# Softmax reciprocals of an attention stage: from TensorE transposes to a VectorE block transpose and a trip through HBM

## The chip, the core and the metric

The kernel runs on one core of a Trainium2 chip. The metric is the device time of one execution in microseconds (us); the number given for a kernel is the median of its runs. The engines are named as the profile names them: PE (TensorE, matrix products and transposes), PEld (its weight loads), DVE (VectorE), ACT (ScalarE), POOL (GpSimd) and SP (SyncE, which here only issues DMAs). PSUM is the memory that TensorE writes to, SBUF the memory of all engines, HBM the memory off the core.

## The reference, cut to what matters

Causal attention over 2 batches of 12 heads (448 tokens, 64 features a head), its output taken as an 896 x 768 matrix into two feed-forward blocks. Of the attention:

```
scores = where(mask, -1e9, scale * q @ k.T)
attn   = exp(scores - max(scores))
attn   = attn / (sum(attn) + 1e-9)
out    = attn @ v
x      = out with the heads side by side      # 896 x 768
```

Then `(sigmoid(x w_gate) * (x w_val)) w_out` (d_ff 1536), and a second block with softmax, a layer norm and two more products. The change touches only the division by `sum(attn) + 1e-9`.

## The kernel before, in words

**Stages.** Attention comes first, then the first feed-forward block (loops over 12 blocks of `d_ff` at L625 and 6 blocks of features at L659), then the second (7 blocks of 128 tokens). All products are of float32 split into a high and a low part, three products for one.

**Attention.** Heads are taken two at a time, 12 pairs. For a pair `p`, PE forms the scores of four query tiles (`sc_mm`, L364: tiles 3 and 0 first, then 2 and 1) in PSUM; DVE takes the row maxima (`sc_max`, L374); ACT takes the exponentials with the row sums in the same instruction (`sc_exp`, L383, line L388 in the profile), each followed by a short instruction that reads the accumulator out. The probabilities `p_t` hold queries on the partitions; PE transposes them in four groups `u` (`tr_mm`, L435, line L439), ACT copies each group to `pt` as the high part (`tr_hi`, L442, line L446) and DVE subtracts to form the low part (`tr_lo`, L448, line L231). PE multiplies with `v` (`pv_mm`, L457, line L470). The result `x` has features on the partitions and queries along the free axis.

**The division.** It is made on that result, so each query's reciprocal has to stand in a row, repeated over the 64 features of its head. POOL adds 1e-9 to the sums (`sums`, L391, line L393), DVE takes the reciprocals of a 128 x 8 block (`recips`, L396), POOL spreads each over 64 columns (`rs_wide`, L401; line L225, tile `rx`), PE transposes the four blocks of 128 x 128 into PSUM (`rs_mm`, L406; line L411, tile `r`), ACT copies them to SBUF (`rs_out`, L413; line L223, tile `rb`), and DVE multiplies (`x_mul`, L474). ACT and POOL then split the product into high and low parts (`x_hi`, `x_lo`).

**What sets the order.** It is written out by hand. `STEPS` (L515) is a table of entries (step, engine, function, and optionally the first pair and the end of the range). One pair begins every 8 steps, and the loop at L578 runs at each step `s` the entries of PE ('E'), then a piece of the first feed-forward block where it can be had (`early_tiles`), then ACT ('A'), DVE ('D') and POOL ('P'), within an engine in the order of the table. An engine executes in this order and waits on semaphores. At one step `s = 8k` DVE meets entries of three pairs: step 16 of pair k-2 (`tr_lo` of group 3), step 0 of pair k (`sc_max` of tiles 3 and 0), and one step later the reciprocals of pair k-1. ACT at that step has `tr_hi` of group 3, `rs_out`, `x_hi`, and at step `8k+1` the exponential of tile 3 of the new pair.

**DMA.** All DMAs are issued by SP, in program order: `load_qk` (two pairs ahead, after POOL's `prep_k_lo`), `load_v` (after `prep_v_lo`), and the weights (`dma_next`) at steps 8 and 12 and again from step 95 on.

Of the kernel before, what the change touches and what calls it, by code (L numbers as in the profile page):

```python
# [10 lines left out]
F32 = mybir.dt.float32  # L11
# [8 lines left out]
B, H, S, D = 2, 12, 448, 64  # L20
# [3 lines left out]
NQ = 4  # L24
QE = [64, 192, 320, 448]
# [7 lines left out]
EPS_SUM = 1e-9  # L33
# [10 lines left out]
def attn_moe_moe2(ctx: ExitStack, tc: tile.TileContext, qk, v, w_gv, w_out, w_in2, w_out2, g_ln, out):  # L44
# [3 lines left out]
    nc = tc.nc  # L48
# [145 lines left out]
    with ExitStack() as actx:  # L194
# [1 line left out]
        qks = actx.enter_context(tc.tile_pool(name="qks", bufs=2, side="right"))  # L196
        one = actx.enter_context(tc.tile_pool(name="one", bufs=1, side="right"))
        ptp = actx.enter_context(tc.tile_pool(name="ptp", bufs=2, side="right"))
        st = actx.enter_context(tc.tile_pool(name="st", bufs=2, side="right"))
        xfp = actx.enter_context(tc.tile_pool(name="xfp", bufs=2, side="right"))  # L200
        ps_t = actx.enter_context(tc.tile_pool(name="ps_t", bufs=2, space=PSUM, reuse_waits="tile"))
        ps_x = actx.enter_context(tc.tile_pool(name="ps_x", bufs=2, space=PSUM, reuse_waits="tile"))
        ps_s = actx.enter_context(tc.tile_pool(name="ps_s", bufs=2, space=PSUM, reuse_waits="tile"))
# [17 lines left out]
        def on(eng, out, in_):  # L221
            if eng == 'A':
                nc.scalar.copy(out=out, in_=in_)  # L223
            elif eng == 'P':
                nc.gpsimd.tensor_scalar(out=out, in0=in_, scalar1=1.0, scalar2=1.0, op0=ALU.mult, op1=ALU.mult)  # L225
            else:
                nc.vector.tensor_copy(out=out, in_=in_)
# [72 lines left out]

        v3 = [one.tile([128, 2, 2 * D], FR, name=f"v3_{i}") for i in range(2)]
        sum_t = [one.tile([128, 16], F32, name=f"sum{i}") for i in range(3)]
        p_t = [one.tile([128, POFF[NQ]], F32, name=f"p{i}") for i in range(2)]

        mx0 = [one.tile([128, 2], F32, name=f"mx{e}") for e in range(2)]
# [19 lines left out]
        load_v(1)  # L325
        zeros(1)

        rs_t, rx_t, rb_t, pt_t, ps_sc, ps_both, ps_tr, ps_pv, ps_rr, xf_t = {}, {}, {}, {}, {}, {}, {}, {}, {}, {}


        def sc_mask(p, g):
# [57 lines left out]
                                         func=AF.Exp, bias=mx, scale=1.0, accum_out=sm)  # L389

        def sums(p):  # L391
            rs = rs_t[p] = st.tile([128, 16], F32, tag="rs", name="rs")
            nc.gpsimd.tensor_scalar(out=rs[:, 8:16], in0=sum_t[p % 3][:, 0:8], scalar1=EPS_SUM, scalar2=0.0,  # L393
                                    op0=ALU.add, op1=ALU.add)

        def recips(p):  # L396
            nc.vector.reciprocal(out=rs_t[p][:, 0:8], in_=rs_t[p][:, 8:16])

        def rs_wide(p):  # L401
            rx = rx_t[p] = st.tile([128, NQ, 2, D], F32, tag="rx", name="rx")
            r = rs_t.pop(p)[:, 0:8].rearrange("p (a i) -> p i a", a=2)
            on('P', rx, r.unsqueeze(3).to_broadcast([128, NQ, 2, D]))

        def rs_mm(p):  # L406
            ps = ps_rr[p] = ps_x.tile([128, 512], F32, tag="x", name="r")[:, :S]
            rx = rx_t.pop(p).rearrange("p i a d -> p i (a d)")
            for i in range(NQ):

                nc.tensor.transpose(ps[:, max(QE[i] - 128, 0):max(QE[i], 128)], rx[:, i], ident if i else identx)  # L411

        def rs_out(p):  # L413
            rb_t[p] = xfp.tile([128, S], F32, tag="rb", name="rb")
            on('A', rb_t[p], ps_rr.pop(p))


        def tr_blocks(u):

# [70 lines left out]
        def early_tiles():  # L490
# [25 lines left out]
            (0, 'E', lambda p: sc_mm(p, (0, 1)), 3), (2, 'E', lambda p: sc_mm(p, (1,)), 2, 3),  # L516
            *((9 + 2 * u, 'E', lambda p, u=u: tr_mm(p, u), int(u < 2)) for u in range(4)),
            *((13 + n, 'E', lambda p, n=n: pv_mm(p, n)) for n in range(len(CHUNKS))),
            (15, 'E', rs_mm),
            (16, 'A', lambda p: tr_hi(p, 3)), (16, 'A', rs_out), (24, 'A', x_hi, 0, NPR - 1), (22, 'A', x_hi, NPR - 1),  # L520
            (1, 'A', lambda p: sc_exp(p, (3,), (0,)), 2),
            (9, 'A', lambda p: tr_hi(p, 0), 1),
            (1, 'A', lambda p: sc_exp(p, (3,), (1,)), 2), (2, 'A', lambda p: sc_exp(p, (0,)), 2),
            (12, 'A', lambda p: tr_hi(p, 1), 1), (5, 'A', lambda p: sc_exp(p, (2,)), 1),
            (14, 'A', lambda p: tr_hi(p, 2)), (6, 'A', lambda p: sc_exp(p, (1,)), 1),
            (-1, 'D', lambda p: sc_max(p, 3, 0), 2, 3),
            (16, 'D', lambda p: tr_lo(p, 3)), (0, 'D', lambda p: sc_max(p, 3, 0), 3),
            (-7, 'D', prep_q_lo, 3), (9, 'D', recips),
            (2, 'D', lambda p: sc_max(p, 2), 2), (11, 'D', lambda p: tr_lo(p, 0), 1), (3, 'D', lambda p: sc_max(p, 1), 2),
            (13, 'D', lambda p: tr_lo(p, 1)), (21, 'D', x_mul), (15, 'D', lambda p: tr_lo(p, 2)),  # L530
            (8, 'P', sums, 1), (9, 'P', prep_v_lo, 1), (25, 'P', x_lo, 0, NPR - 1), (23, 'P', x_lo, NPR - 1),
            (10, 'P', rs_wide),
            (-10, 'P', prep_k_hi, 3), (-9, 'P', prep_q_hi, 3), (-4, 'P', prep_k_lo, 3), (7, 'P', prep_v_hi, 1),
        )

        sc_mm(0, (0, 1))
# [41 lines left out]
        for s in range(PER * NPR + 26):  # L578
            steps(s, 'E')
            for _ in range(2):  # L580
                if s >= PER * NPR and left and next(early):
                    left -= 1
            steps(s, 'A')
            steps(s, 'D')
            steps(s, 'P')
            if s in (8, 12):
                dma_next()

            for c in range(2 * NE + 2):
                e = s - 88 - 8 * c  # L590
                if e in (3, 5, 7):
                    next(bits_now)
                if e == 8 and c < 2 * NE:
                    chunk_hi(c)
                if e == 9 and c < 2 * NE:
                    chunk_lo(c)
                if e == 0:
                    bits_now = bits_steps(c)
                    next(bits_now)
# [237 lines left out]
```

## Time and profile before

| | |
|---|---|
| median of 3 runs (lowest, highest) | 493.98 us (493.77, 493.98) |
| the profiled execution, its own time | 493.84 us |
| its span, first to last instruction | 492.1 us |
| PE busy, share of the span | 486.2 us, 99% |
| DVE, ACT, POOL busy | 329.0, 225.7, 125.4 us |
| granted TensorE clock, mean | 1.000 |
| DMA packets, data | 12996, 52.79 MB |

The span leaves out some 1.7 us of the execution's own time. A busy PE is a PE with at least one matmul in flight by the profile's model of their ends, so 99% does not say that PE is what the rest waits for; that has to be read from the waits. The attention stage takes the first 105 us or so.

### The profile page before, as it was taken

The page shows a single profiled execution, that of the slowest core. Times are in us where ns is not written, and L with a number is a line of the kernel's source. Part 1 is how long each engine was busy: PE and PEld are TensorE (multiplying, and loading weights), DVE is VectorE, ACT ScalarE, POOL GpSimd, SP SyncE. Part 2 cuts the span into 40 slices and gives each one's busy share as a digit, 9 for nine tenths or more (in the row PEclk, how much of TensorE's full clock was granted, in tenths as well). Part 3 has the DMA queues.
Part 4 walks back from the last instruction along what each step waited for, and adds up shares of the span by engine and source line. Part 5 has one row for each costly group of instructions (what it writes and reads, how often), then busy time and mean ns, then how long its engine had stood idle before and what let it go on. Part 6 is the DMA issues. An engine that isn't in the chain of part 4 may idle for free.

```text
span 492.1 us, 7603 instructions
## 1 busy us (share of the span) xinstructions
PE 486.2 (99%) x2955; PEld 445.6 (91%) x2955; DVE 329.0 (67%) x496; ACT 225.7 (46%) x483; POOL 125.4 (25%) x200
## 2 busy tenths in 40 slices
PE   8999999999999999999999999999999999999997
PEld 7998999899999999999999999999988888899996
DVE  7898888986656778877777746767735987821110
ACT  6988989853433543453453332343321434323111
POOL 5888877610000000000000000000060778510000
PEclk9999999999999999999999999999999999999999
DMA  6722330223332454443344334443331121001001
GB/s 191 249 83 97 93 107 23 65 78 121 124 129 59 156 170 132 168 155 111 121 170 143 114 107 138 162 157 120 132 127 56 74 78 52 1 33 64 33 33 64
DMA packets 12996, 52.79 MB, mean 107 GB/s; under 512 B 1568, under 2 KB 2080, under 8 KB 12960
## 3 DMA queue, kind: packets, MB, share of 16 engines
q1 hardware_dynamic: 12960, 52.31, 32.2%
q8 instruction: 23, 0.38, 0.3%
q14 instruction: 13, 0.11, 0.1%
HBM read 49.55 MB, written 2.75 MB: 106 GB/s over the span
## 4 chain that ended last, share of the span: by engine, by line
PE 82%; ACT 12%; DVE 3%; issue 2%; DMA 1%; POOL 0%; SPq 0%; ACTq 0%; DVEq 0%
PE gv L643 34%; PE pm L673 18%; PE po L766 12%; PE h L705 12%; ACT p L388 7%; ACT pt L446 4%; DVE sum L376 1%; PE gv L502 1%; PE tp L748 1%; DVE pt L231 1%; PE x L470 1%; DMA qkr<-in_qk_dram 1%; PE t L439 1%; PE s L361 1%; PE warm L315 0%
## 5 line engine op out<-in xcount | busy, mean ns | idle before, releaser
L643 PE MATMUL gv<-xy,hl 128*128 128x448 f32 x828 | 168.1, 365 | 0.0
L643 PEld LDWEIGHTS gv<-xy,hl 128*128 128x128 f32 x828 | 155.4, 188 | 12.3
L673 PE MATMUL pm<-g,hl 128*128 128x448 f32 x432 | 87.7, 365 | 0.0
L673 PEld LDWEIGHTS pm<-g,hl 128*128 128x128 f32 x432 | 81.1, 188 | 6.4
L690 POOL TENSOR_SCALAR t<-t,g_sb 128x768 f32<-128x768 f32 x8 | 9.0, 1130 | 247.7 <-PE pm L673 247.7
L134 DVE TENSOR_TENSOR hl<-t,hl 128x768 fp32r<-128x768 f32 x36 | 35.1, 975 | 41.7 <-ACT hl L131 40.0
L766 PE MATMUL po<-wo,lt 128*128 128x384 f32 x336 | 60.6, 339 | 0.0
L705 PE MATMUL h<-wi,xy 128*128 128x512 f32 x252 | 59.3, 396 | 0.0
L766 PEld LDWEIGHTS po<-wo,lt 128*128 128x128 f32 x336 | 58.7, 188 | 0.2 <-POOL wo L695 0.2
L705 PEld LDWEIGHTS h<-wi,xy 128*128 128x128 f32 x252 | 47.1, 187 | 11.4
L117 DVE SCALAR_TENSOR_TENSOR t<-raw,t 128x768 int32<-128x768 int32 (+1 forms) x56 | 52.6, 939 | 1.8
L120 DVE SCALAR_TENSOR_TENSOR t<-raw,t 128x768 int32<-128x768 int32 (+1 forms) x56 | 52.0, 929 | 1.7
L112 ACT ACTIVATE raw<-raw 128x768 f32<-128x768 f32 (+1 forms) x56 | 48.1, 867 | 9.5 <-DMA raw<-in_wo_dram 6.4
L470 PE MATMUL x<-pt,v 128*128 128x384 f32 (+3 forms) x252 | 51.3, 325 | 0.0
L388 ACT ACTIVATE p<-s,sum 128x320 f32<-128x320 f32 (+3 forms) x92 | 43.7, 495 | 10.0 <-DVE sum L376 9.7
L231 DVE TENSOR_TENSOR pt<-t,pt 128x512 fp32r<-128x512 f32 (+1 forms) x48 | 32.2, 671 | 11.2 <-ACT pt L446 11.0
L470 PEld LDWEIGHTS x<-pt,v 128*128 128x128 f32 x252 | 36.9, 190 | 1.6
L171 DVE TENSOR_TENSOR lt<-tp,lt 128x512 fp32r<-128x512 f32 x14 | 9.7, 690 | 36.4 <-ACT lt L170 36.4
L115 DVE TENSOR_SCALAR t<-raw 128x768 int32<-128x768 int32 (+1 forms) x56 | 30.6, 547 | 3.0 <-ACT raw L112 3.0
L131 ACT CAST hl<-t 128x768 fp32r<-128x768 f32 x36 | 30.0, 833 | 4.2 <-PE pm L673 4.2
L183 ACT ACTIVATE wk<-gv 128x448 f32<-128x448 f32 x23 | 11.3, 542 | 44.5 <-PE gv L643 44.5
L446 ACT CAST pt<-t 128x512 fp32r<-128x512 f32 (+1 forms) x48 | 28.3, 590 | 3.1 <-PE t L439 3.1
(101 smaller groups left out, 523.7 us busy)
## 6 DMA issues: line engine op xcount, KB each, us to landing
raw<-in_gv_dram SPq DMA_DIRECT2D x24, 768.0 KB, 4.4
raw<-in_wo_dram SPq DMA_DIRECT2D x20, 768.0 KB, 4.4
raw<-in_wi_dram SPq DMA_DIRECT2D x12, 512.0 KB, 3.5
qkr<-in_qk_dram SPq DMA_DIRECT2D x11, 448.0 KB, 3.3
vr<-in_v_dram SPq DMA_DIRECT2D x12, 256.0 KB, 2.7
out_dram<-o SPq DMA_DIRECT2D x6, 384.0 KB, 2.3
qkr<-in_qk_dram SPq DMA_DIRECT2D x2, 224.0 KB, 2.8
out_dram<-o SPq DMA_DIRECT2D x2, 192.0 KB, 1.9
```

The lines of the kernel that those rows point to most:

```text
L112: nc.scalar.activation(out=w1.bitcast(F32), in_=w1.bitcast(F32), func=AF.Copy, scale=2.0 ** -112)
L117: nc.vector.scalar_tensor_tensor(out=tt, in0=w1, scalar=-2 ** 31, in1=tt, op0=ALU.bitwise_and, op1=ALU.bitwise_or)
L120: nc.vector.scalar_tensor_tensor(out=tt, in0=w0, scalar=29, in1=tt, op0=ALU.logical_shift_right, op1=ALU.bitwise_or)
L134: nc.vector.tensor_tensor(out=lo, in0=t_t.pop(it), in1=f32(hi), op=ALU.subtract)
L231: (nc.gpsimd if eng == 'P' else nc.vector).tensor_tensor(out=out, in0=a, in1=b, op=ALU.subtract)
L388: nc.scalar.activation(out=p_t[p % 2][:, POFF[i] + (1 - e) * n:POFF[i] + (2 - e) * n], in_=ps_sc[p, i][1 - e], func=AF.Exp, bias=mx, scale ...
L446: nc.scalar.copy(out=pt_t[p][:, 0, u, :w], in_=ps_tr[p, u][:, :w])
L470: nc.tensor.matmul(out=ps[:, q0:], lhsT=l, rhs=pt_t[pr][:, c, u, c0:c0 + S - q0], start=(chunk == 0 and n == 0), stop=(chunk == 7 and n == ...
L643: nc.tensor.matmul(out=ps[i, b], lhsT=w[:, a, cs], rhs=xy[kk][:, x, b * S:(b + 1) * S], start=(kk == 0 and a == 0 and x == 0), stop=(kk == ...
L673: nc.tensor.matmul(out=ps[b], lhsT=w[:, a, cs], rhs=g_t[kk][:, x, b * S:(b + 1) * S], start=(kk == 0 and a == 0 and x == 0), stop=(kk == N ...
L705: nc.tensor.matmul(out=h[:, n * 512:(n + 1) * 512], lhsT=xy[kk][:, a, tk], rhs=wi[n * NK + kk][:, c], start=(kk == 0 and i == 0), stop=(kk ...
L766: nc.tensor.matmul(out=ps[n], lhsT=lts[k // 4][:, a, k % 4], rhs=wo[k][:, c, cs], start=(k == 0 and i == 0), stop=(k == NF2 - 1 and i == 2))
```

## The change

It leaves out `rs_wide`, `rs_mm` and `rs_out`, and with them the tiles `rx` and `r` and ACT's copy from `r` to `rb`. In their place DVE, right behind the reciprocal, transposes a 128 x 32 block (8 columns of reciprocals, 24 of zeros) in four blocks of 32 x 32. Row c of each 32-row block then holds the reciprocals of column c for 32 queries. SP writes them to an HBM tile of 8 rows of 128 floats, one DMA for each block (8 rows of 128 bytes), and reads the tile back with two DMAs, one for each head of the pair, each the same 448 floats to 64 partitions. `rb` is written by these DMAs. In `STEPS`, `recips` moves from step 9 to step 8 and to the front of DVE's entries there, so that it stands ahead of `tr_lo` of group 3; `sums` moves from step 8 to the end of step 7 on POOL, which leaves POOL's order as it was; and a new engine key 'S' for SP runs behind DVE and ahead of POOL at each step.

```diff
-        st = actx.enter_context(tc.tile_pool(name="st", bufs=2, side="right"))
+        drm = actx.enter_context(tc.tile_pool(name="drm", bufs=2, space=bass.MemoryType.DRAM))
...
+        rs_in, rs_t, rs_q = ([one.tile([128, n], F32, name=f"rs{n}{o}{i}") for i in range(2)]
+                             for n, o in ((8, "i"), (32, "t"), (32, "q")))
+        for i in range(2):
+            nc.gpsimd.memset(rs_t[i], 0.0)
...
         def sums(p):
-            rs = rs_t[p] = st.tile([128, 16], F32, tag="rs", name="rs")
-            nc.gpsimd.tensor_scalar(out=rs[:, 8:16], in0=sum_t[p % 3][:, 0:8], scalar1=EPS_SUM, scalar2=0.0,
+            nc.gpsimd.tensor_scalar(out=rs_in[p % 2], in0=sum_t[p % 3][:, 0:8], scalar1=EPS_SUM, scalar2=0.0,
                                     op0=ALU.add, op1=ALU.add)
 
         def recips(p):
-            nc.vector.reciprocal(out=rs_t[p][:, 0:8], in_=rs_t[p][:, 8:16])
-
-
-
-        def rs_wide(p):
-            rx = rx_t[p] = st.tile([128, NQ, 2, D], F32, tag="rx", name="rx")
-            r = rs_t.pop(p)[:, 0:8].rearrange("p (a i) -> p i a", a=2)
-            on('P', rx, r.unsqueeze(3).to_broadcast([128, NQ, 2, D]))
-
-        def rs_mm(p):
-            ps = ps_rr[p] = ps_x.tile([128, 512], F32, tag="x", name="r")[:, :S]
-            rx = rx_t.pop(p).rearrange("p i a d -> p i (a d)")
-            for i in range(NQ):
-
-                nc.tensor.transpose(ps[:, max(QE[i] - 128, 0):max(QE[i], 128)], rx[:, i], ident if i else identx)
-
-        def rs_out(p):
+            nc.vector.reciprocal(out=rs_t[p % 2][:, 0:8], in_=rs_in[p % 2])
+            nc.vector.transpose(out=rs_q[p % 2], in_=rs_t[p % 2])
+
+        def rs_rows(p):
+            rows = rd_t[p] = drm.tile([2 * NQ, 128], F32, tag="rd", name="rd")
+            for b in range(0, 128, 32):
+                nc.sync.dma_start(out=rows[:, b:b + 32], in_=rs_q[p % 2][b:b + 8])
+
+        def rs_bcast(p):
             rb_t[p] = xfp.tile([128, S], F32, tag="rb", name="rb")
-            on('A', rb_t[p], ps_rr.pop(p))
-
+            rows = rd_t.pop(p).rearrange("(a i) r -> a (i r)", a=2)[:, D:]
+            for a in range(2):
+                nc.sync.dma_start(out=rb_t[p][a * D:(a + 1) * D], in_=rows[a:a + 1].to_broadcast([D, S]))
...
-            (15, 'E', rs_mm),
-            (16, 'A', lambda p: tr_hi(p, 3)), (16, 'A', rs_out), (24, 'A', x_hi, 0, NPR - 1), (22, 'A', x_hi, NPR - 1),
+            (16, 'A', lambda p: tr_hi(p, 3)), (24, 'A', x_hi, 0, NPR - 1), (22, 'A', x_hi, NPR - 1),
...
-            (16, 'D', lambda p: tr_lo(p, 3)), (0, 'D', lambda p: sc_max(p, 3, 0), 3),
-            (-7, 'D', prep_q_lo, 3), (9, 'D', recips),
+            (8, 'D', recips), (16, 'D', lambda p: tr_lo(p, 3)), (0, 'D', lambda p: sc_max(p, 3, 0), 3),
+            (-7, 'D', prep_q_lo, 3),
...
-            (8, 'P', sums, 1), (9, 'P', prep_v_lo, 1), (25, 'P', x_lo, 0, NPR - 1), (23, 'P', x_lo, NPR - 1),
-            (10, 'P', rs_wide),
-            (-10, 'P', prep_k_hi, 3), (-9, 'P', prep_q_hi, 3), (-4, 'P', prep_k_lo, 3), (7, 'P', prep_v_hi, 1),
+            (9, 'P', prep_v_lo, 1), (25, 'P', x_lo, 0, NPR - 1), (23, 'P', x_lo, NPR - 1),
+            (8, 'S', rs_rows), (9, 'S', rs_bcast),
+            (-10, 'P', prep_k_hi, 3), (-9, 'P', prep_q_hi, 3), (-4, 'P', prep_k_lo, 3), (7, 'P', prep_v_hi, 1), (7, 'P', sums, 1),
...
             steps(s, 'D')
+            steps(s, 'S')
             steps(s, 'P')
```

## Rows read from the trace of the kernel before

**Rows 1.** The page: busy time of each engine, share of the span.

```profile
PE 486.2 (99%) x2955; PEld 445.6 (91%) x2955; DVE 329.0 (67%) x496; ACT 225.7 (46%) x483; POOL 125.4 (25%) x200
```

**Rows 2.** The waits: us in total, times, longest us.

```profile
ACT p L388 <- DVE sum L376: 9.7, 9, 1.1
...
ACT p L388 <- DVE rs L397: 0.3, 1, 0.3
```

**Rows 3.** The chain of waits, 46.5 to 50 us: start us, us, what.

```profile
47.10 0.64 DVE pt L231
```

**Rows 4.** The timeline of ACT, one turn: start us, us, ... [idle before <-releaser].

```profile
46.37 0.22 ACT L388 ACTIVATION_READ_ACCUMULATOR p<-s,sum 128x1 f32 x1
46.46 0.60 ACT L446 CAST pt<-t 128x512 fp32r<-128x512 f32 x1
46.93 0.57 ACT L223 COPY rb<-r 128x448 f32<-128x448 f32 x1
...
49.10 0.64 ACT L388 ACTIVATE p<-s,sum 128x448 f32<-128x448 f32 x1 [1.14 <-DVE sum L376]
```

**Rows 5.** The timeline of DVE, the same turn.

```profile
47.10 0.69 DVE L231 TENSOR_TENSOR pt<-t,pt 128x512 fp32r<-128x512 f32 x1 [0.60 <-ACT pt L446]
47.71 1.28 DVE L376 TENSOR_REDUCE sum<-s 128x2 f32<-128x896 f32 x2
48.91 1.11 DVE L252 SCALAR_TENSOR_TENSOR qks<-qkr,qks 128x448 fp32r<-128x448 f32 x1
49.95 0.19 DVE L397 RECIPROCAL rs<-rs 128x8 f32<-128x8 f32 x1
50.06 0.77 DVE L376 TENSOR_REDUCE sum<-s 128x2 f32<-128x640 f32 x1
```

**Rows 6.** The timeline of POOL, the same turn.

```profile
46.67 0.26 POOL L393 TENSOR_SCALAR rs<-sum 128x8 f32<-128x8 f32 x1 [0.60 <-ACT p L388]
47.01 1.44 POOL L231 TENSOR_TENSOR v<-vr,v 128x384 fp32r<-128x384 f32 x2
48.40 1.14 POOL L231 TENSOR_TENSOR xy<-xf,xy 128x448 fp32r<-128x448 f32 x1
```

**Rows 7.** The timeline of PE, the same turn.

```profile
45.90 0.27 PE L411 MATMUL r<-identx,rx 128*128 128x128 f32 x1
...
46.43 0.26 PE L348 MATMUL s<-mk_r,mk_l 64*128 64x64 bf16 x6
```

**Rows 8.** The timeline of PE, the last pair's transposes.

```profile
100.42 0.27 PE L411 MATMUL r<-identx,rx 128*128 128x128 f32 x1
...
100.77 0.65 PE L502 MATMUL gv<-xy,hl 128*128 128x448 f32 x2
```

**Rows 9.** The timeline of DVE in the second block: two short dependent instructions.

```profile
392.42 0.14 DVE L719 TENSOR_SCALAR st<-st 128x1 f32<-128x1 f32 x1
392.59 0.16 DVE L720 RECIPROCAL st<-st 128x1 f32<-128x1 f32 x1
```

**Rows 10.** Groups of DVE's instructions by line, 0 to 140 us: count | busy us, mean ns.

```profile
L288 DVE CAST mk_l<-two 128x64 bf16<-128x64 f32 x1 | 0.2, 195 | 0.0
```

**Rows 11.** The timeline of DVE, pair 0: its reciprocal and its multiplication.

```profile
14.15 0.19 DVE L397 RECIPROCAL rs<-rs 128x8 f32<-128x8 f32 x1
...
21.25 0.61 DVE L476 TENSOR_TENSOR xf<-x,rb 128x448 f32<-128x448 f32 x1
22.76 0.69 DVE L231 TENSOR_TENSOR pt<-t,pt 128x512 fp32r<-128x512 f32 x1 [0.90 <-ACT pt L446]
```

**Rows 12.** The timeline of SP's queue: the first two weight loads.

```profile
14.15 0.90 SPq L100 DMA_DIRECT2D raw<-in_gv_dram  x2
```

**Rows 13.** The page's DMA issues: count, KB each, us to landing.

```profile
raw<-in_gv_dram SPq DMA_DIRECT2D x24, 768.0 KB, 4.4
...
vr<-in_v_dram SPq DMA_DIRECT2D x12, 256.0 KB, 2.7
...
out_dram<-o SPq DMA_DIRECT2D x2, 192.0 KB, 1.9
```

More of the change, by code (lines that the diff above doesn't have):

```diff
@@ L326, in attn_moe_moe2 @@
         zeros(1)
-        rs_t, rx_t, rb_t, pt_t, ps_sc, ps_both, ps_tr, ps_pv, ps_rr, xf_t = {}, {}, {}, {}, {}, {}, {}, {}, {}, {}
+        rd_t, rb_t, pt_t, ps_sc, ps_both, ps_tr, ps_pv, xf_t = {}, {}, {}, {}, {}, {}, {}, {}
         def sc_mask(p, g):
```

## The prediction

> **What bounds the kernel now.** The page comes first: PE is busy for 99% of the span [rows 1], so taking four transposes a pair off it looks like a gain. But that counts a matmul as busy until its modelled end, so I went to the waits. In the attention stage it is not PE that others wait for: the wait that returns is ACT's exponential, 9.7 us in 9 waits for DVE's maxima and a tenth for DVE's reciprocal [rows 2]. The chain of waits then runs over DVE and ACT alone between 46.5 and 50 us; DVE's subtraction for `pt` (L231, `tr_lo` of group 3) stands on it [rows 3].
>
> One turn, read off the timelines. ACT's cast of group 3 runs from 46.46 to 47.06; DVE has been idle for 0.60 us for it and starts `tr_lo` at 47.10, then the maxima of the next pair's tiles 3 and 0 (47.71 to 48.99), and ACT, idle for 1.14 us, starts that pair's exponentials at 49.10 [rows 4, 5]. From there to the next cast of group 3 ACT is in one piece. So a turn is ACT's run plus the 2.0 us of DVE between cast and exponential; there are ten, one for each of pairs 2 to 11, one for each of the ten waits [rows 2]. `rb`'s copy stands between the cast and ACT's 1.14 us of idle time [rows 4] and only shortens the latter, and the chain never meets the transposes. Whatever goes onto DVE between 47.06 and 49.10 lengthens the turn; what leaves PE, ACT or POOL doesn't shorten it.
>
> Now what the moved reciprocal waits for. ACT has read out the last sum at 46.59; POOL waited 0.60 us for that and adds the epsilon from 46.67 to 46.93 [rows 4, 6]. So the sums reach DVE inside its idle 0.60 us, but near its end.
>
> **The change part by part.**
>
> *Removed.* Four transposes a pair on PE, 0.53 us from the first to the next matmul (45.90 to 46.43) [rows 7]; the copy on ACT, 46.93 to the next start at some 47.4 [rows 4]; the spreading on POOL. In the turns all of these cost or give nothing: ACT waits for DVE behind them anyway, DVE's maxima start as `tr_lo` lets them, and POOL idles ahead of its sums. If PE's cover went, the maxima at 47.71 would wait for the scores; with less work on PE they come earlier. In the last pair PE runs without a pause and its four transposes hold it from 100.42 to 100.77 [rows 8]: -0.35 us.
>
> *Moved: the reciprocal, to the front of DVE's entries at step 8k, and added: the block transpose.* The hand-over between engines takes 0.04 (ACT to DVE, 47.06 to 47.10) to 0.08 us (ACT to POOL, 46.59 to 46.67) [rows 4, 5, 6]; with 0.06 the reciprocal starts at 46.99 and ends 0.19 later, at 47.18 [rows 5]. The transpose reads what it wrote; of two such dependent instructions the second starts 0.03 us after the first's end (392.56 to 392.59) [rows 9], so 47.21. How long a block transpose holds DVE no row shows. A reciprocal of 8 columns lets the next instruction go 0.11 us after its start (49.95 to 50.06) [rows 5], a cast of 64 columns takes 0.195 in all [rows 10]. The transpose has 32 columns. I take 0.11, because between 8 and 64 columns the whole duration hardly changes, and keep as ends 0.11 with no wait for the reciprocal at all and 0.30 (the cast and half as much again for filling a block before it drains). `tr_lo` then starts at 47.21 + 0.11 = 47.32 instead of 47.10: **+0.22 us a turn** (ends +0.11: 46.99 + 0.22 = 47.21; and +0.41). Ten turns: +2.2 us (+1.1 to +4.1). By the Trainium skill (VectorE: DVE Perf Modes, The three transpose paths) VectorE takes 311 ns for 128 x 128 of bf16 in such blocks; less 96 columns that is an estimate of 0.21 us in all, 0.13 to the next start, and the sum would be 0.2 us higher; no row here shows one.
>
> Behind the moved instructions on DVE wait `tr_lo`, both maxima and through them ACT's exponential, which is what I have counted. Where the reciprocal stood before, DVE gains 0.11 us [rows 5]. That is beside ACT's run, except in the last turn, where the exponential was released by the reciprocal [rows 2]: -0.1 us.
>
> In the first turn DVE is late by pair 0's transpose (its reciprocal ends at 14.34 with DVE's next work close behind [rows 11]) rather than by pair 1's; I count it once.
>
> *Added: six DMAs a pair on SP.* SP issues a DMA every 0.45 us when nothing holds it [rows 12]: four writes 1.8 us, two reads 0.9. No DMA here writes 128-byte rows; the nearest small one, 192 KB out, lands 1.9 us after its issue, and the largest, a weight load, after 4.4 us [rows 13]. These are my ends, and I take 2.2 for landing, near the smaller. A read of `rb` is 115 KB, two together about a `v` load, 2.7 us [rows 13]. From the transpose's end at 47.4: 1.8 + 2.2 + 0.9 + 2.7 puts `rb` in place at about 55.0 (at most 57.2), and `x_mul` of that pair comes 13 steps behind its reciprocal, where a turn has 8. From the transposes of pair 4 at 45.90 to those of pair 11 at 100.42 [rows 7, 8] there are seven turns of 7.8 us; 13 steps are 12.7 us, so `x_mul` comes past 59. Hidden, cost 0. The loads of `v` and of q and k queue behind the reads' wait on SP, some 3 us later than now; they are used a turn or more after they land.
>
> The tight place is pair 0: 14.6 + 7.6 = 22.2, with a weight load put between the writes and the reads on SP, against `x_mul` at 21.25; but DVE then idles 0.90 us, to 22.76 [rows 11], and again ahead of `tr_lo`. So 0, at most +1 us once.
>
> **The sum.** 2.2 - 0.35 - 0.1 = +1.75 us on the profiled execution of 493.84 (492.1 of span and 1.7 around it), 495.6. That execution lies 0.14 under the median; on the median it is 495.7. The ends: 1.1 - 0.45 = +0.65, 494.6; 4.1 - 0.45 + 1 = +4.65, 498.6.
>
> **The rivals.**
>
> *PE is the bound after all.* For it speaks the 99% [rows 1]. Then 12 x 0.53 = 6.4 us go, 487.6. Against it: ACT waits in each turn for DVE, and DVE for ACT [rows 4, 5]; neither waits for PE. It decides where DVE's maxima wait for scores. The scores follow PE's transposes at once [rows 7], so there is little room; but for a gain the `tr_lo` in front of the maxima would have to be early, and it isn't moved. Chance 0.10.
>
> *The two instructions fit into the 0.60 us.* If the sums come some 0.2 us earlier than I read, nothing is added to a turn and only the tail's 0.45 us is left: 493.5, no difference that can be seen. ACT's read-out ends at 46.59 and the epsilon at 46.93 [rows 4, 6], which leaves 0.17 of the 0.60 us; a reciprocal alone takes longer. Chance 0.13.
>
> *The block transpose is locked out by POOL.* POOL and DVE do block each other: DVE's L252 takes 1.11 us, and it begins at 48.91 while POOL subtracts `xy` until 49.54 [rows 5, 6]; less that wait of 0.63 it needs 0.48. POOL's subtraction for `v` starts at 47.01, just ahead of the transpose, two operations to 48.45, the first (L266) with 384 columns, the second (L267) with 128 [rows 6], so that the first ends near 48.09. A transpose that waits for it goes there, lets DVE on at 48.20, and `tr_lo` 1.1 us late instead of 0.22: ten turns, +10.5 us, 504.5. It decides from the moment that the transpose begins after POOL. By the Trainium skill (SBUF — State Buffer, SBUF: two separate sides) the port pair that the two share is held by one for a whole instruction, on DVE's side by those with two SBUF inputs or in a two-port mode; this fits L252, which has two, and the transpose would be caught only if it ran in such a mode. Against it: the transpose has one input, as the reciprocal has. Chance 0.05.
>
> **How the numbers follow.** My case has 0.72: +0.65 to +4.65, likeliest 495.7. About 0.2% (1.0 us) is what a measurement of this kernel can tell from no change. Of the 0.72, 0.05 lie below that (transpose at the cheap end), so slower is 0.67 + 0.05 of the lock = 0.72; same 0.13 + 0.05 = 0.18; faster 0.10. The range takes my case from 493.9, where most of the no-change case joins, up to 498.2, which leaves out the lock, the PE case and the dearest end.
>
> **What would show it.** In the profile after: the reciprocal near 47.0 of a turn and a transpose behind it, both inside what was the 0.60 us wait, with `tr_lo` no longer preceded by idle time for ACT; ACT idle ahead of the exponential for some 1.8 us instead of 1.14 (some 0.4 of it the copy's, 0.22 the two instructions'); no wait of `x_mul` for a DMA past pair 0; PE with more gaps and no shorter stage. Wrong, if a turn is shorter than before, if the transpose lasts over 0.5 us, if DVE's multiplication waits for `rb` in each turn, or if SP's queue makes POOL wait for q and k.

## The result, and the profile after

| | before | after |
|---|---|---|
| median of the runs (lowest, highest) | 493.96 us (493.77, 493.98) | 496.61 us (496.06, 497.47) |
| ratio, 95% interval | | 1.0056 [1.0039, 1.0074] |
| the profiled execution, its own time | 493.84 us | 496.59 us |
| its span | 492.1 us | 494.7 us |

The changed kernel is slower by some 0.56%, 2.65 us between the medians. The forecast was 495.7 us with a range of 493.9 to 498.2. What follows uses the profiled executions, whose spans differ by 2.6 us.

The page of the changed kernel, busy time by engine:

```profile
PE 483.2 (98%) x2907; PEld 439.6 (89%) x2907; DVE 329.6 (67%) x508; ACT 221.0 (45%) x471; POOL 121.0 (24%) x190
```

Against [rows 1] PE has 48 matmuls fewer and 3.0 us less to do, ACT 4.7 and POOL 4.4 us less. DVE has 12 more instructions and 0.6 us more. Three engines were relieved, and the kernel is slower.

The waits of the changed kernel from 0 to 115 us (us in total, times, longest us) say on whom the work now stands:

```profile
ACT p L392 <- DVE sum L380: 16.7, 10, 3.0
...
POOL qks L225 <- DMA qkr<-in_qk_dram: 8.5, 4, 4.0
...
PE t L435 <- DVE pt L231: 4.5, 11, 1.5
...
DVE xf L472 <- DMA rb<-rd: 1.0, 1, 1.0
```

ACT's wait ahead of the exponentials grew from 9.7 us [rows 2] to 16.7. PE, now with less to do, waits for DVE, and POOL waits 8.5 us for q and k. In the kernel before that last wait is 4.8 us, all of it in the first 10 us; of the 8.5, only 4.0 fall there.

One turn on DVE, the changed kernel's timeline:

```profile
48.91 0.20 DVE L400 RECIPROCAL rs32t<-rs8i 128x8 f32<-128x8 f32 x1 [0.45 <-POOL rs8i L396]
49.15 0.21 DVE L401 STREAM_TRANSPOSE rs32q<-rs32t 128x32 f32<-128x32 f32 x1
49.28 0.65 DVE L231 TENSOR_TENSOR pt<-t,pt 128x512 fp32r<-128x512 f32 x1
49.85 1.28 DVE L380 TENSOR_REDUCE sum<-s 128x2 f32<-128x896 f32 x2
51.04 0.92 DVE L252 SCALAR_TENSOR_TENSOR qks<-qkr,qks 128x448 fp32r<-128x448 f32 x1
```

and on ACT:

```profile
48.37 0.65 ACT L442 CAST pt<-t 128x512 fp32r<-128x512 f32 x1
...
51.24 0.64 ACT L392 ACTIVATE p<-s,sum 128x448 f32<-128x448 f32 x1 [1.75 <-DVE sum L380]
...
53.48 0.61 ACT L442 CAST pt<-t 128x512 fp32r<-128x512 f32 x1
53.95 0.57 ACT L392 ACTIVATE p<-s,sum 128x320 f32<-128x320 f32 x1
```

This answers to [rows 4, 5]. DVE no longer waits for ACT ahead of `tr_lo` (L231); it waits for POOL's sums, then does the reciprocal and the transpose. From ACT's cast of group 3 to the exponential it was 49.10 - 46.46 = 2.64 us and is 51.24 - 48.37 = 2.87: +0.23.

A turn is counted from the first 128x448 exponential of a pair to that of the next (pair 11's is the last); "rest" is the span less the last of these, so what follows the loop:

| kernel | to pair 2 | to pair 3 | to pair 4 | to pairs 5 to 11 | last start | rest |
|---|---|---|---|---|---|---|
| before | 5.86 | 8.54 | 7.68 | 7 x 7.68 | 87.52 | 404.6 |
| after | 5.44 | 9.07 | **9.15** | 7 x **7.87** | 90.59 | 404.1 |

The first of these exponentials starts at 11.66 before and 11.85 after. So the 3.07 us by which pair 11 comes later are 0.19 of start, 0.11 over the turns to pairs 2 and 3, 1.47 in the one to pair 4, and 7 x 0.19 = 1.3. The start is no cost of the change: in the kernels below it lies between 11.49 and 11.86, and it is 11.83 in e8, whose edit touches only later pairs. The tail gives 0.4 to 0.5 back (the spans are given to 0.1 us).

**The long turn.** The chain of waits of the changed kernel (start, us, what) goes through a load before it comes to DVE's added work:

```profile
27.18 3.65 DMA qkr<-in_qk_dram
...
30.98 0.04 POOL qks L225
...
33.17 0.21 DVE rs32t L400
```

SP's queue in the timeline, and below it SP's own wait for the rows (us in total, times, longest us), show why that q and k load is so late:

```profile
18.74 0.59 SPq L100 DMA_DIRECT2D raw<-in_gv_dram  x1
19.37 1.34 SPq L406 DMA_DIRECT2D rd<-rs32q  x4
25.34 1.09 SPq L412 DMA_DIRECT2D rb<-rd  x2
26.54 0.53 SPq L219 DMA_DIRECT2D vr<-in_v_dram  x1
27.18 0.36 SPq L214 DMA_DIRECT2D qkr<-in_qk_dram  x1
```

```profile
SPq L412 <- DMA rd<-rs32q: 22.3, 14, 4.5
```

In the kernel before, SP issues the same load, and POOL uses it, at

```profile
20.81 0.33 SPq L214 DMA_DIRECT2D qkr<-in_qk_dram  x1
```

```profile
28.87 0.57 POOL L225 TENSOR_SCALAR qks<-qkr 128x448 fp32r<-128x448 f32 x1
```

There it lands 4.3 us after its issue, at 25.1, and has 3.8 us to spare. In the changed kernel it is issued 6.4 us later.

The four writes of pair 1 are issued right behind a 768 KB weight load. SP's next entry, the reading back, has to wait for them, from 20.71 on and for 4.5 us, and issues at 25.34. The loads of v and of q and k stand behind it; q and k are issued at 27.18 and land at 30.83 (27.18 + 3.65). The profile's chain names an instruction of DVE as what released this issue (L252, which ends at 27.09); e4 below rules that out. On POOL the late load becomes a gap:

```profile
26.55 1.54 POOL L231 TENSOR_TENSOR qks<-qkr,qks 128x448 fp32r<-128x448 f32 x1
30.98 0.56 POOL L225 TENSOR_SCALAR qks<-qkr 128x448 fp32r<-128x448 f32 x1 [2.89 <-DMA qkr<-in_qk_dram]
...
32.90 0.24 POOL L396 TENSOR_SCALAR rs8i<-sum 128x8 f32<-128x8 f32 x1
```

POOL works in order, so the sums (L396) come only after that load has been split, and DVE's reciprocal, which now stands ahead of `tr_lo` and the maxima, waits for the sums. The chain runs on to the exponential at 35.51.

### The profile page after: what moved, and what is told of

Its sections match the earlier page's. It is cut to its first block, busy times and chain, and to the rows that moved or that the text cites. A ratio compares the mean times of both kernels' runs of the same rounds, so it can differ in the third digit from the quotient of the medians.

```text
span 494.7 us, 7578 instructions
## 1 busy us (share of the span) xinstructions
PE 483.2 (98%) x2907; PEld 439.6 (89%) x2907; DVE 329.6 (67%) x508; ACT 221.0 (45%) x471; POOL 121.0 (24%) x190
## 4 chain that ended last, share of the span: by engine, by line
PE 81%; POOL 5%; DMA 5%; issue 3%; DVE 2%; ACT 2%; SPq 1%; POOLq 0%; ACTq 0%
PE gv L639 34%; PE pm L669 18%; PE po L762 12%; PE h L701 12%; DMA qkr<-in_qk_dram 3%; PE gv L498 2%; DMA rd<-rs32q 2%; PE tp L744 1%; POOL qks L231 1%; ACT p L392 1%; PE x L466 1%; POOL v L225 1%; POOL v L231 1%; POOL xy L231 1%; DVE pt L231 1%
## 5 line engine op out<-in xcount | busy, mean ns | idle before, releaser
L120 DVE SCALAR_TENSOR_TENSOR t<-raw,t 128x768 int32<-128x768 int32 (+1 forms) x56 | 52.0, 929 | 1.7
L392 ACT ACTIVATE p<-s,sum 128x320 f32<-128x320 f32 (+3 forms) x92 | 44.4, 510 | 16.7 <-DVE sum L380 16.7
L231 DVE TENSOR_TENSOR pt<-t,pt 128x512 fp32r<-128x512 f32 (+1 forms) x48 | 31.7, 660 | 6.7 <-ACT pt L442 6.5
L435 PE MATMUL t<-ident,p 128*128 128x128 f32 x180 | 28.5, 279 | 4.4 <-DVE pt L231 3.3
```

The lines of the kernel that those rows point to most:

```text
L120: nc.vector.scalar_tensor_tensor(out=tt, in0=w0, scalar=29, in1=tt, op0=ALU.logical_shift_right, op1=ALU.bitwise_or)
L231: (nc.gpsimd if eng == 'P' else nc.vector).tensor_tensor(out=out, in0=a, in1=b, op=ALU.subtract)
L392: nc.scalar.activation(out=p_t[p % 2][:, POFF[i] + (1 - e) * n:POFF[i] + (2 - e) * n], in_=ps_sc[p, i][1 - e], func=AF.Exp, bias=mx, scale ...
```

## The experiments

The theories that the expectations name: **A**, mine: DVE's instructions between ACT's cast and the exponential set a turn, and SP's wait for the rows holds up loads. **B**: PE's work sets the turn. **C**: the trip through HBM itself is what costs. **D**: the reciprocals fit into DVE's wait for ACT. **E**: the rows disturb the loads wherever they are issued. **F**: PE sets the turn once it is relieved. All results first; the turns are read as above, from one profiled execution each.

| kernel | median us (lowest, highest) | ratio to before, 95% | to pair 2 | 3 | 4 | 5 to 11 | rest |
|---|---|---|---|---|---|---|---|
| e1 relief only | 493.33 (493.12, 493.41) | 0.9986 [0.9977, 0.9995] | 5.44 | 8.67 | 7.68 | 7.68 | 404.1 |
| e2 DVE's part | 495.98 (495.86, 496.08) | 1.0040 [1.0026, 1.0053] | 5.86 | 8.94 | 7.88 | 7.87 | 404.6 |
| e3 move only | 494.07 (494.01, 494.17) | 1.0001 [0.9993, 1.0010] | 5.86 | 8.55 | 7.69 | 7.68 | 404.6 |
| e4 weights later | 495.82 (495.25, 496.47) | 1.0037 [1.0025, 1.0050] | 5.44 | 9.06 | 7.87 | 7.87 | 404.2 |
| e5 reciprocals later | 496.91 (496.59, 498.64) | 1.0065 [1.0053, 1.0077] | 5.44 | 10.82 | 7.68 | 7.68; two of 7.86, 7.99 | 405.3 |
| e6 both | 494.96 (493.85, 496.31) | 1.0023 [1.0011, 1.0036] | 5.44 | 8.86 | 7.68 | 7.68; one of 8.30 | 405.3 |
| e7 maximum first | 494.16 (492.81, 496.23) | 1.0007 [0.9997, 1.0016] | 5.44 | 8.42 | 7.67 | 7.31 to 7.88 | 405.2 |
| e8 before, maximum first | 493.86 (493.82, 493.99) | 0.9998 [0.9990, 1.0007] | 5.86 | 8.24 | 7.88 | 7.69 | 404.6 |
| e9 queue, maximum first | 493.70 (493.55, 495.12) | 1.0001 [0.9992, 1.0010] | 5.43 | 8.43 | 7.66 | 7.62 | 405.2 |
| e10 queue only | 496.61 (496.53, 496.82) | 1.0056 [1.0044, 1.0069] | 5.44 | 10.82 | 7.87 | 7.87 | 404.1 |
| e11 queue, reciprocals | 494.55 (494.30, 494.57) | 1.0013 [1.0004, 1.0022] | 5.43 | 8.87 | 7.67 | 7.67 | 405.3 |
| e12 order | 492.07 (491.99, 492.14) | 0.9960 [0.9946, 0.9974] | 5.44 | 9.04 | 7.49 | 7.50, last 7.31 | 404.2 |

### Is PE the bound? (e1)

```diff
-            (15, 'E', rs_mm),
-            (16, 'A', lambda p: tr_hi(p, 3)), (16, 'A', rs_out), (24, 'A', x_hi, 0, NPR - 1), (22, 'A', x_hi, NPR - 1),
+            (16, 'A', lambda p: tr_hi(p, 3)), (24, 'A', x_hi, 0, NPR - 1), (22, 'A', x_hi, NPR - 1),
...
-            (10, 'P', rs_wide),
...
-            nc.vector.tensor_tensor(out=xf, in0=ps_pv.pop(pr), in1=rb_t.pop(pr), op=ALU.mult)
+            nc.vector.tensor_tensor(out=xf, in0=ps_pv.pop(pr), in1=ones, op=ALU.mult)
```

> The kernel before without the transposes of the sums and their spreading matmuls on TensorE; the output is multiplied by a tile of ones, so the division by the sums is left out. Theory A (VectorE's chain sets the turn, TensorE only waits less or more): the turns stay at 7.68 us from one first exponential to the next, and only the tail gets shorter, by 0.4 to 0.5: 493.4 to 493.6 us. Rival B (TensorE's work sets the turn, so its relief is worth some 0.5 us a turn): about 488 us.

Eight turns stay at 7.68 and the rest is 0.4 to 0.5 shorter: 493.33 us, just under A's range. Theory B falls for this order of the work. The relief (of PE, and with it of ACT and POOL) is worth 0.65 us when nothing is paid for it.

### What DVE's part costs (e2, e3)

e2 against before; e3 is e2 without the line of the transpose:

```diff
-            nc.vector.reciprocal(out=rs_t[p][:, 0:8], in_=rs_t[p][:, 8:16])
+            nc.vector.reciprocal(out=rs_32[p % 2][:, 0:8], in_=rs_in[p % 2])
+            nc.vector.transpose(out=rs_q[p % 2], in_=rs_32[p % 2])
...
-            (16, 'D', lambda p: tr_lo(p, 3)), (0, 'D', lambda p: sc_max(p, 3, 0), 3),
-            (-7, 'D', prep_q_lo, 3), (9, 'D', recips),
+            (8, 'D', recips), (16, 'D', lambda p: tr_lo(p, 3)), (0, 'D', lambda p: sc_max(p, 3, 0), 3),
+            (-7, 'D', prep_q_lo, 3),
...
-            (8, 'P', sums, 1), (9, 'P', prep_v_lo, 1), (25, 'P', x_lo, 0, NPR - 1), (23, 'P', x_lo, NPR - 1),
+            (9, 'P', prep_v_lo, 1), (25, 'P', x_lo, 0, NPR - 1), (23, 'P', x_lo, NPR - 1),
...
-            (-10, 'P', prep_k_hi, 3), (-9, 'P', prep_q_hi, 3), (-4, 'P', prep_k_lo, 3), (7, 'P', prep_v_hi, 1),
+            (-10, 'P', prep_k_hi, 3), (-9, 'P', prep_q_hi, 3), (-4, 'P', prep_k_lo, 3), (7, 'P', prep_v_hi, 1), (7, 'P', sums, 1),
```

> The kernel before with the reciprocals where the change puts them, ahead of tr_lo(3), and the block transpose behind them (into a tile that nothing reads); TensorE's transposes and matmuls stay, no row goes to HBM. Theory A: each turn 0.19 us longer (7.87), ten turns, no tail saved and no late load: 1.5 to 2.0 above before, 495.5 to 496.0 us, and the turn from pair 0 to pair 1 is no longer than the others. Rival C (the trip through HBM is what costs): within 0.3 of before, 494.0 us.

> As e2_dve_part without the block transpose: the reciprocals alone are moved ahead of tr_lo(3). Theory A, where the reciprocal's 0.19 and the transpose's 0.13 both lie on the chain and some 0.1 of slack is had back: 7.72 to 7.78 a turn, 494.3 to 495.0 us. Rival D (the reciprocals fit into the 0.60 us that tr_lo(3) waits for ScalarE, and the transpose alone costs): 7.68 a turn, 493.9 to 494.1 us.

e2 gives all of the 0.19 a turn, and neither a long turn nor a shorter rest: 495.98 us, with no DMA of the change in it. Theory C can't be the whole. The medians add up: e2 costs 2.00 us and e1 gains 0.65, which leaves 1.30 of the 2.65 us for what neither has, the trip through HBM, and the long turn of the changed kernel is 9.15 - 7.87 = 1.28 too long. In e3 the cost is gone, as theory D has it. The timeline of DVE in e3 shows how near that is:

```profile
47.07 0.20 DVE L400 RECIPROCAL rs32t<-rs8i 128x8 f32<-128x8 f32 x1 [0.46 <-POOL rs8i L396]
47.20 0.69 DVE L231 TENSOR_TENSOR pt<-t,pt 128x512 fp32r<-128x512 f32 x1
```

ACT's cast began at 46.51 there, so `tr_lo` starts 0.69 us behind it where it was 0.64 [rows 4, 5]: 0.05 late. The turn gets that back elsewhere. In the kernel before, ACT's timeline has

```profile
51.34 0.61 ACT L446 CAST pt<-t 128x512 fp32r<-128x512 f32 x1
51.85 0.53 ACT L388 ACTIVATE p<-s,sum 128x320 f32<-128x320 f32 x1
```

and DVE's has

```profile
51.28 0.54 DVE L376 TENSOR_REDUCE sum<-s 128x2 f32<-128x384 f32 x1
```

It is 0.51 us from the cast to the next exponential, and 0.47 in the changed kernel (53.48 to 53.95 above). By the times, the exponential waits there for DVE's second maximum behind the old place of the reciprocal, which ends at 51.82, 0.03 ahead of it; with the reciprocal gone from there it no longer waits 0.04. So a turn is +0.23 less 0.04, and the block transpose alone makes it dear.

### The long turn (e4, e10)

```diff
-            if s in (8, 12):
+            if s in (28, 36):
```

> The changed kernel with the two weight loads of a turn issued at steps in the second half of the turn (29 to 36 in place of 9 to 12), so that the rows of 128 bytes are not queued on SP and the rings behind a bulk load. Theory A (the one long turn of 9.15 us comes from SP waiting for these rows with the q and k loads queued behind): that turn is 7.9, the rest stay 7.87, 495.2 to 495.5 us. Rival C (the rows' landing itself is slow, whatever stands ahead of them): the 4.9 us landing and the long turn stay, 496.6 us.

In the profiled run of e4 the long turn is gone and everything else is as in the changed kernel; 495.30 us, its own time, is what theory A had. The load of q and k is issued at 24.04, two microseconds before DVE's L252 begins (26.08), so L252 is not what it waits for. But the five runs are 1.2 us apart and their median, 495.82, is above theory A's range, so in others something still came late. SP's waits did not go either: up to 4.0 us in this trace, for rows behind the moved weight loads (rows issued at 40.16 behind a load of 39.36, read back at 45.58). POOL then waits 0.71 us for q and k, once, and no turn is longer for it.

e10 leaves the weights alone and moves the reading back behind the q and k load:

```diff
-            (8, 'S', rs_rows), (9, 'S', rs_bcast),
+            (8, 'S', rs_rows), (13, 'S', rs_bcast),
```

> The changed kernel with one edit: the reading back is issued at step 13 in place of 9, so that it comes behind the q and k load of the turn on SP and no load stands behind its wait for the rows; the weight loads stay where they were. Theory A (what is lost beyond VectorE's 0.19 a turn is q and k loads queued behind that wait, in some runs more than in others): all turns 7.87, none longer, 495.0 to 495.5 us, and the runs within 0.5 us of each other (e4_weights_later: 1.2 apart). Rival E (the rows take the rings' time from the loads, wherever they are issued): a long turn stays in most runs, 496 to 497 us, over 1 us apart.

This missed. The turn to pair 4 is 7.87, but the one before it is now 10.82. SP's queue and DVE in e10:

```profile
16.33 0.83 SPq L100 DMA_DIRECT2D raw<-in_gv_dram  x2
18.32 1.14 SPq L412 DMA_DIRECT2D rb<-rd  x2
```

```profile
24.29 0.62 DVE L472 TENSOR_TENSOR xf<-x,rb 128x448 f32<-128x448 f32 x1 [2.42 <-DMA rb<-rd]
```

Pair 0's reading back now stands behind two weight loads and `x_mul` of pair 0 waits 2.42 us for it. The 496.61 us lie in rival E's range, but not by its mechanism: the runs are 0.3 us apart, and the one long turn has one wait in it. So theory A was too narrow: what hurts is a small transfer that somebody waits for behind a bulk load, be the waiter SP (with loads behind it) or DVE. The Trainium skill (DMA: Bandwidth & Descriptors, Queues, rings and completion order) says that each DMA engine takes its ring's work in order and that a completion is only signalled after every earlier write of that DMA engine. The trace agrees: in the changed kernel SP waited 4.5 us for the rows right behind the weight load of 18.74, and such a load takes 4.3 us on that kernel's page; it waited 2.6 us for rows right behind the loads of v and of q and k (issued from 27.60 to 28.94, read back at 31.57), and 1.0 us where the last load was issued 3 us earlier (57.26 to 58.56, read back at 59.58).

### Both terms away (e5, e6, e11)

e5 takes the reciprocals to a place where ACT is busy, e6 adds the later weights:

```diff
-            (8, 'D', recips), (16, 'D', lambda p: tr_lo(p, 3)), (0, 'D', lambda p: sc_max(p, 3, 0), 3),
+            (16, 'D', lambda p: tr_lo(p, 3)), (0, 'D', lambda p: sc_max(p, 3, 0), 3),
...
-            (2, 'D', lambda p: sc_max(p, 2), 2), (11, 'D', lambda p: tr_lo(p, 0), 1), (3, 'D', lambda p: sc_max(p, 1), 2),
+            (2, 'D', lambda p: sc_max(p, 2), 2), (11, 'D', lambda p: tr_lo(p, 0), 1), (3, 'D', lambda p: sc_max(p, 1), 2), (11, 'D', recips),
...
-            (8, 'S', rs_rows), (9, 'S', rs_bcast),
+            (11, 'S', rs_rows), (12, 'S', rs_bcast),
```

> The changed kernel with the reciprocals and the block transpose behind the second maximum of the next score tile (where VectorE no longer delays an exponential), the writing and the reading back of the rows three steps later. Theory A: turns of 7.63 to 7.70 us, the late q and k load perhaps still there (+1.3), tail about as in the changed kernel: 493.3 to 495.0 us. Rival C (the trip through HBM costs, not VectorE's place): a later trip makes the product with the spread reciprocals wait more, 497 us or above.

> e5_recips_later with the weight loads of e4_weights_later. Theory A, both terms taken away and the tail kept: turns of 7.65, no long turn, 493.2 to 493.6 us, some 0.1% under before. Rival C: 496 us or above.

The turns are 7.68 again where no load is late. The times missed. Most of it in e5 is the turn of 10.82: pair 0's reading back came late there as in e10, and `x_mul` waited for it (the wait in us in total, the number of such waits in the first 115 us, the longest):

```profile
DVE xf L472 <- DMA rb<-rd: 2.9, 1, 2.9
```

Two more reasons hold for both kernels. First, the late loads came oftener: the reading back now stood just ahead of the q and k load. SP in e6, and POOL after it:

```profile
42.23 0.43 SPq L100 DMA_DIRECT2D raw<-in_gv_dram  x1
42.70 0.42 SPq L219 DMA_DIRECT2D vr<-in_v_dram  x1
44.00 1.62 SPq L406 DMA_DIRECT2D rd<-rs32q  x4
50.13 1.09 SPq L412 DMA_DIRECT2D rb<-rd  x2
51.31 0.54 SPq L214 DMA_DIRECT2D qkr<-in_qk_dram  x1
```

```profile
56.09 0.57 POOL L225 TENSOR_SCALAR qks<-qkr 128x448 fp32r<-128x448 f32 x1 [3.16 <-DMA qkr<-in_qk_dram]
```

Second, the rest is 405.3 instead of 404.1, of which below. e11 is e6 with the reading back at step 13, behind the q and k load, and the weights one step later:

> e6_both with the reading back at step 13 (behind the q and k load) and the weight loads a step later. Theory A, both terms gone and the shorter tail kept: turns of 7.68, 493.3 to 493.7 us, runs within 0.5 us. Rival E: as e6_both, 494 to 496 us, runs 2 us apart.

All turns are 7.67, no wait of POOL for q and k is left past the start, and eleven runs lie within 0.27 us, where e6's six lay 2.5 apart. That is theory A's claim shown, and E falls: the same rows and the same loads, in an order in which no q and k load stands behind the wait. The median of 494.55 is in E's range all the same; it missed A's by the 1.2 us of the rest.

### Where the tail went, and a better order (e7 to e9, e12)

e7 is e6 with two neighbours exchanged on DVE, e8 the same exchange alone in the kernel before:

```diff
-            (16, 'D', lambda p: tr_lo(p, 3)), (0, 'D', lambda p: sc_max(p, 3, 0), 3),
+            (0, 'D', lambda p: sc_max(p, 3, 0), 3), (16, 'D', lambda p: tr_lo(p, 3)),
```

> e6_both with the first maximum of the next pair's score tile 3 ahead of tr_lo(3) on VectorE: tr_lo(3) waits for ScalarE in each turn, and the maximum could use that wait, if TensorE has the scores by then. If the relieved TensorE has them (theory A, TensorE has slack now): 7.2 to 7.4 a turn, 489 to 491 us. If not (rival B, TensorE is as late as VectorE): 7.68 or more, 493.5 us or above.

> The kernel before with the same exchange as e7_max_first (maximum of score tile 3 ahead of tr_lo(3)), the control for it. Theory A: TensorE's extra transposes and matmuls make the scores later, the gain is smaller than in e7_max_first: 491 to 494 us. Rival: the exchange does the same with and without TensorE's relief, and the change gives nothing: as e7_max_first plus 0.4 of tail.

e8 gains nothing, and its waits, 40 to 90 us, say why:

```profile
DVE sum L376 <- PE s L361: 7.5, 7, 1.1
```

With the maximum ahead, DVE stands waiting for PE's scores, some 1.1 us a turn, and a turn is 7.69: what PE needs for its own work, to within the 0.2 us by which DVE's `pt` still comes late for it. So, by these waits, two bounds lay side by side in the kernel before, DVE's chain at 7.68 and PE at 7.5 to 7.69, and neither e1 nor e8 could shorten a turn by lifting one. e7 lifts both and has turns of 7.31, but others of up to 7.88, and its twelve runs spread over 3.4 us: the late loads again (POOL waits for q and k in six turns). Its 494.16 us are rival B's time, its turns of 7.31 theory A's. e9 is e7 with e11's queue:

> e7_max_first with the reading back at step 13 (behind the q and k load) and the weight loads a step later. e7_max_first showed turns of 7.31 us where no load was late and TensorE without a wait in them. Theory A: the turns from pair 1 on are 7.3 to 7.5 us, 490.2 to 491.8 us, 0.5% under before, runs within 0.6 us. Rival E: the late loads stay, 493 to 495 us, runs over 2 us apart.

The loads are on time and most runs agree, two of eleven excepted; the turns are 7.62, not 7.4, the rest is still 405.2, and 493.70 us misses A's range. The tail's loss stands in e11's trace on DVE, POOL and PE in turn:

```profile
93.23 1.67 DVE L120 SCALAR_TENSOR_TENSOR t<-raw,t 128x768 int32<-128x768 int32 x1
```

```profile
93.08 2.13 POOL L231 TENSOR_TENSOR v<-vr,v 128x384 fp32r<-128x384 f32 x2
```

```profile
95.82 0.68 PE L498 MATMUL gv<-xy,hl 128*128 128x448 f32 x2 [1.17 <-ACT hl L131]
```

L120 prepares the first weight chunk that PE multiplies in the tail. In the kernel before, DVE and POOL had

```profile
93.01 0.95 DVE L120 SCALAR_TENSOR_TENSOR t<-raw,t 128x768 int32<-128x768 int32 x1
```

```profile
93.10 2.15 POOL L231 TENSOR_TENSOR v<-vr,v 128x384 fp32r<-128x384 f32 x2
```

The moved reciprocals (0.37 us on DVE with the transpose, 89.70 to 90.07 in e11) had pushed L120 from just before to just after the start of POOL's subtraction; it then took 1.67 us, and PE waited 1.17 us for the chunk. e12 moves the reciprocals ahead of `tr_lo(0)`, where DVE waits for ACT, and L252 away from POOL's subtractions:

```diff
-            (0, 'D', lambda p: sc_max(p, 3, 0), 3), (16, 'D', lambda p: tr_lo(p, 3)),
-            (-7, 'D', prep_q_lo, 3),
-            (2, 'D', lambda p: sc_max(p, 2), 2), (11, 'D', lambda p: tr_lo(p, 0), 1), (3, 'D', lambda p: sc_max(p, 1), 2), (11, 'D', recips),
+            (8, 'D', recips, 11), (0, 'D', lambda p: sc_max(p, 3, 0), 3), (16, 'D', lambda p: tr_lo(p, 3)),
+            (2, 'D', lambda p: sc_max(p, 2), 2), (10, 'D', recips, 0, 11), (11, 'D', lambda p: tr_lo(p, 0), 1), (3, 'D', lambda p: sc_max(p, 1), 2),
+            (-5, 'D', prep_q_lo, 3),
```

> e9_queue_max with VectorE's order changed at two places: the q low part (L252) comes behind the second maximum, so that it doesn't begin while GpSimd runs a tensor_tensor (in e9_queue_max it took 0.92 us in place of 0.61), and the reciprocals come ahead of tr_lo(0), which waits for ScalarE, so that in the last turn the first weight chunk is no later than in the kernel before (in e9_queue_max its L120 began behind GpSimd's tensor_tensor, took 1.50 in place of 0.95 us, and TensorE waited 0.99 for that chunk). Theory A (these two collisions hold what the relieved TensorE could give): turns of 7.3 to 7.5 us and a tail 1.0 shorter, 490.0 to 491.8 us, 0.4 to 0.8% under both kernels. Rival F (TensorE's own work sets e9_queue_max's turn): turns stay at 7.6, only the tail is won, 492.6 to 493.0 us.

```profile
91.57 0.95 DVE L120 SCALAR_TENSOR_TENSOR t<-raw,t 128x768 int32<-128x768 int32 x1
```

```profile
91.62 2.19 POOL L231 TENSOR_TENSOR v<-vr,v 128x384 fp32r<-128x384 f32 x2
```

```profile
93.44 0.68 PE L498 MATMUL gv<-xy,hl 128*128 128x448 f32 x2 [0.42 <-ACT hl L131]
```

Begun 0.05 us before POOL, L120 takes 0.95 us, PE waits 0.42, and the rest is 404.2. From the last pair's exponential to this product of PE it is 8.30 us in e11, 7.39 in e12 and 7.36 in the kernel before: 0.9 of the tail's 1.1 us, 0.75 of them this wait; the last 0.2 are not accounted for. The turns are 7.50, at the upper end of what A had, with DVE waiting 1.0 us in each for PE's scores and L252 still at 0.77 to 0.80 us. The turn to pair 3 is 0.6 longer than in e9, for a cause that stays open, and with it the time is 0.3 above A's range. e12 takes 492.07 us, ratio 0.9960 [0.9946, 0.9974]: 1.95 us below the kernel before of its own comparison (494.02) and some 4.5 below the changed one. Its order of DVE and its later weight loads were not tried on the kernel before, so how much of the 1.95 us they would give without the relief is not shown; e8, where DVE waits 1.1 us a turn for PE, speaks against a shorter turn there.

## Why the prediction was right, and where not

- **What bounds the kernel.** Right for the order at hand: e1. The rival that PE is the bound lost, but it was nearer than its text said: e8 puts PE's turn at up to 7.69 against DVE's 7.68. "ACT waits in each turn for DVE" showed which of the two came last, not by how much.
- **+0.22 us a turn.** From the cast to the exponential it measured +0.23, a turn +0.19. The step that failed by 0.04 is "where the reciprocal stood before, DVE gains 0.11 us ... beside ACT's run": ACT's run held a wait of 0.04 for it. The transpose held DVE 0.13 us (49.15 to 49.28) where I took 0.11 from the reciprocal. By the Trainium skill (VectorE: DVE Perf Modes, The three transpose paths) the estimate was 0.21 in all and 0.13 to the next start, and the trace has just these two numbers.
- **The tail, -0.35 and -0.1.** Measured: 404.6 to 404.1, so -0.4 to -0.5. The sum was right and its second term was not. e1, with the reciprocal in its old place, has the whole gain; e2 and e3, with it moved, keep 404.6. The last exponential starts 0.11 us after the maxima end (86.13 + 1.28 to 87.52), as in every turn [rows 4, 5], so the reciprocal that the profile names there held up nothing. The relief gave all of it, where the transposes were put at 0.35.
- **Ten turns alike.** The first two were not: together +0.11 instead of +0.44. Over these two e1 is 0.29 shorter (0.42 off the turn to pair 2, 0.13 back in the next) and e2 0.40 longer, which makes the +0.11. So the difference comes from the relief, at a place where my PE term was zero. Pair 0's `x_mul` did wait 0.97 us for `rb`, but it cost nothing that shows: the sum comes out of e1 and e2, which have no such DMA, and the 0.90 us for which DVE idled behind `x_mul` [rows 11] are gone. That part of the DMA term was right.
- **The DMAs at 0, "at most +1 us once".** This is the term that was mis-sized, and it was at another place than forecast. The failed step is "the loads of `v` and of q and k queue behind the reads' wait on SP ...; they are used a turn or more after they land". In the kernel before, the load of q and k had 3.8 us to spare, half a turn, and it came 6.4 us later, not "some 3". It landed at 30.83 and POOL had been idle for it since 28.09 (26.55 + 1.54). It cost 1.47 - 0.19 = 1.28 us in the profiled execution, and e4, e6 and e11 tie it to SP's wait. I had taken 2.2 us for the rows' landing, near the smaller of two ends (1.9 and 4.4); behind a bulk load SP waited 4.5, over the larger, and with none just ahead 1.0. The prediction had named this as a sign of being wrong: "if SP's queue makes POOL wait for q and k". That sign came. Of its other signs, only the turn to pair 2 was shorter than before; the transpose took 0.21 us and `x_mul` waited for `rb` once.
- **The sum.** 1.75 was forecast and 2.6 measured on the span. The late load adds 1.28, the start 0.19; the first two turns (0.33) and the smaller turn (8 x 0.03) take 0.6 off, and the tail is as forecast to 0.05: 1.75 + 1.47 - 0.6 = 2.6. That the forecast of 495.7 came within 0.9 us of 496.61 is in part luck: a late load put at nothing was half covered by turns put too long.
- **The rivals.** "Fit into the 0.60 us" is true of the reciprocal alone to 0.05 us (e3) and false with the transpose (e2). The lock by POOL fell: the transpose began at 49.15, while POOL subtracted from 48.95 on, and took 0.21.

## What to carry to other kernels

Relief of the busiest engine shortens no turn where another chain is as long (7.68 against up to 7.69 here); look for the second bound before counting it, and lift both (e12), since neither alone shortened a turn. The trip through HBM cost less here by its own latency than by what stood around it in the issuing queue: keep waits for small transfers behind the loads that others need, and small transfers out from behind bulk ones. Work added to an engine should go where it already waits, and a shift of 0.3 us can push another instruction into a collision far from the edit.

## What the runs showed of the hardware

- A VectorE instruction with two SBUF inputs that begins just after a GpSimd tensor_tensor is held while that runs: L120 takes 0.95 us when begun 0.05 before it (e12), 1.67 when begun 0.15 after (e11) and 1.50 when begun 0.31 after (e9), so that in the last two it ends 1.8 us after GpSimd's start. The other way round GpSimd is held (2.19 us in e12 for two subtractions that take 1.42 in the changed kernel, at 48.95). The Trainium skill (SBUF — State Buffer, SBUF: two separate sides) describes a lock of this kind, taken by whichever begins first; these traces agree. The 32-bit block transpose, which has one input, was not held (0.21 us, begun 0.20 after GpSimd's).
- The changed kernel's runs were 1.4 us apart (496.06 to 497.47) where the kernel before had 0.2; e11's queue order brings that to 0.27. A spread that comes with a change can itself point to a queue.
- Open: which of e4's runs had a late transfer and which, since only one of the five has a trace; and why two of e9's eleven runs took 1.4 us more.
